# A new order for the first stage of a windowed-attention and feed-forward kernel: loads that wait for operations, short PE fills, casts on GpSimd, dilated parts split by chunk, and the last product cut in halves

## The chip, the cores and the metric

One core of one Trainium2 chip runs the whole program. The metric is the device time of one execution in microseconds (us). Three runs of the kernel before gave 823.49, 824.78 and 825.17 us, so the median is 824.78 us.

## The reference

The program computes attention inside windows and feeds its result through one gated layer.

```python
# q, k, v: 8 batches, 8 heads, 576 positions, 64 wide; float32
scores = (q @ k.T) / sqrt(64)
# heads 0-3: a query sees its own and the 31 positions before it ("plain")
# heads 4-7: it sees every 4th position among the last 128 ("dilated")
attn = softmax(where(mask, scores, -1e9)) @ v
x = attn.transpose(0, 2, 1, 3).reshape(4608, 512)
h = x @ w_in                       # 512 x 2048
g = h * clip(h + 3, 0, 6) / 6
out = g @ w_out                    # 2048 x 512
```

All products need more than one pass of a 32-bit float, so each of x, g, w_in and w_out is split into a high and a low part (an `fp32r` cast and a subtraction), and each product is the sum of high*high, high*low and low*high.

## The kernel before, in words

The attention is cut into 48 pieces, called trios here, t = 0 to 47. A trio holds 12 blocks of 32 queries of one batch, of plain or of dilated heads. For a trio the steps are: load its keys and queries (k) and its values (v); scores on TensorE (B); the row maximum (R), the subtraction (S) and the exponential (X); a transpose on TensorE (E) and its copy to SBUF (CA); the product with the values, which rides in a later B (FOLLOW, line 57: B3 carries the values of trio 1, B4 of 2, B5 of 3, B7 of 5, B8 of 6) or stands alone (V); the division by the row sum (Z, lines 327 to 341); a transpose back (Y) and its copy (CX, lines 389 to 394); and the split into high (XH, lines 468 to 474) and low parts (XL, lines 476 to 484). A column of tokens called a chunk has 384 of them. A plain trio is half of a chunk's plain heads; a dilated trio covers a third of the batch and so its results lie in several chunks, every fourth column (`spans`, lines 435 to 447).

Four chunks (0 to 3) go through an ordinary feed-forward: G is the first product of one chunk and one 128-wide slice f of the hidden layer (lines 563 to 575, 12 matmuls of 384 columns), RE and T the gate, GH and GL its high and low parts, H the second product (lines 625 to 637, 9 matmuls of 512 columns). The weights arrive as 64-bit numbers (w, one load for w_in and one for w_out of each f) and are converted by seven steps: U and Q on ScalarE, s, j and a on VectorE, h (the high part, lines 548 to 551) on ScalarE and l (the low part) on VectorE. The other tokens go through a scheme of fewer, larger products (lines 639 on), whose order a planner makes (`_in_time`, lines 1369 to 1471) from costs and due times.

The change is almost wholly in the first stage, whose order is written out by hand: the string ORDER (lines 58 to 80). Each word is one step, such as `B4` or `w0@R1`, and the four engines and the load queue that SyncE issues on each do their steps in the order of the string. `@R1` makes a load wait until that step is done (lines 1311 to 1315). ScalarE, VectorE and SyncE are held to the program's order (lines 1303 to 1305), TensorE too. G0, the first product of the feed-forward, can start when trios 0 to 4 are split and the first weights are converted.

D in the string is a fill: n products of zeros that nobody reads, each a float32 matmul of 384 columns, which keep TensorE at work where a wait is expected (lines 184 to 187). Eight bf16 products of zeros (lines 179 to 180) stand ahead of everything. The mask and a small 0/1 matrix come in one load, M0 (lines 799 to 803); every B begins with a matmul that reads both (line 355). A tile for k or v of trios 0 to 8 takes a slot of the general pool (lines 204 to 208).

At the other end, the last product of the last group (T4 in lines 1288 to 1294) is taken row block by row block: the last two of its sixteen steps run for rows 0 to 127 and then for rows 128 to 255, and each half is scaled by ScalarE (line 1150) and sent (line 1190).

```python
        if masked:
            _, kind, part = trios[ts]
            one, rows = (ident_b, P) if ts >= NFIRST else (spread, QB)
            nc.tensor.matmul(ps[:, :CH], lhsT=one, rhs=mask_of(kind, part, rows), start=True, stop=False)
```

Of the kernel before, what the change touches and what calls it, by code (L numbers as in the profile page):

```python
# [74 lines left out]
Q21 GL14 U21 j13 j12 G24 a13 RE7 a12 h13 T7 h12 l13 w22@l20 H14 GH7 RE24 l12 GL7 T24 G17 s21 Q22 j21 GH24 U22 GL24 a21
U23 G16 RE17 s22 s23 h21 T17 j22 GH17 G9 l21 w24@l12 Q24 a22 U24 j23 h22 H24 s24 l22 j24 w25@l22 a23 H15 RE16 GL17 h23
a24 RE9 T16 h24 l23 G26 GH16 T9 Q25 GL16 U25 l24 w27@GH16 GH9 s25 G19 j25 a25 H17 h25 Q27 l25 H16 RE26 GL9 w26@H17 k12
k13 v12 v13 M1 RE19 T26 T19 G21 GH26 GH19 Q26 H9 U26 s26 U27 j26 H7 RE21 GL26 a26 T21 h26 GL19 H5 GH21 l26 GL21 s27
j27 G23 a27 h27 H21 l27 RE23 T23 GH23 H19 GL23 H23
# [7 lines left out]
def windowed_attention_ffn(ctx: ExitStack, tc: tile.TileContext, qk, vp, w, mask, out, out_t):  # L87
# [100 lines left out]


    kqs, vs = {}, {}  # L190
    last = {}
    plan = []

    def in_turn(ins):

        for name in last.values():
            tc.add_manual_dep(
                ins.ins, name, mybir.DependencyInfo(mybir.DependencyClass.NoSync, mybir.DependencyReason.DATA), reason="in turn"
            )
# [10 lines left out]
    def load_qk(t):  # L210
        if t < T and t not in kqs:
            kqs[t] = load_tile(t, "kq", KW + CH)
            ins = nc.sync.dma_start(out=kqs[t], in_=qk[t].rearrange("h d x -> (h d) x"))
            if not plan:
                in_turn(ins)
            return ins
# [94 lines left out]
    def share(t):  # L311
        pv = pvs[t][:, : SLOTS * W].rearrange("p (s x) -> p s x", x=W)
        z = small.tile([P, SLOTS], F32, name="z")
        nc.vector.tensor_scalar_add(z, pv[:, :, D], 1e-9)
        nc.vector.reciprocal(z, z)
        pvs[t] = pv, z

    def shares(t, j):
# [5 lines left out]
        for i in (2 * j, 2 * j + 1):  # L324
            nc.scalar.mul(xs[t][:, i * D : (i + 1) * D], pv[:, i, 0:D], z[:, i : i + 1])
# [20 lines left out]
    def block(ts, tv, pools=()):  # L346
# [21 lines left out]
        last["block"] = product.ins.name  # L368
        return product

    def turn(src):
        ps = ps_a.tile([P, 512], F32, name="ps_a")
        for r in range(RT):
            ins = nc.tensor.transpose(ps[:, r * P : (r + 1) * P], src[:, r * P : (r + 1) * P], ident)  # L374
# [6 lines left out]
    def turn_x(t):  # L381
        tps["x", t], ins = turn(xs.pop(t))
        return ins
# [4 lines left out]

    def turned_x(t):
        xfs[t] = work_tile("xf")  # L390
        return nc.scalar.copy(
            xfs[t].rearrange("p (u i x) -> p i u x", u=2, x=QB),
            tps.pop(("x", t))[:, :CH].rearrange("p (i u x) -> p i u x", u=2, x=QB),
        )
# [73 lines left out]
    def high(t):  # L468
        b, kind, part = trios[t]
        assert b >= PLAIN or all(read[c] == NF for c in chunks(b - 2, kind, part) if b < 2 or c < PLAIN - 2)  # L470
        for src, view, plain in pieces_of(t):
            if plain:
                ins = nc.scalar.copy(view(xh), src)
# [34 lines left out]
    def load_w(p):  # L508
# [4 lines left out]
        in_turn(ins)  # L513
# [17 lines left out]
    def cv_shift(p):  # L531
        v = parts(p)[2]
        return nc.vector.tensor_scalar(
# [14 lines left out]
    def cv_high(p):  # L548
# [1021 lines left out]
```

## Time and profile before

| | |
|---|---|
| median of three runs | 824.78 us |
| the profiled execution | 829.52 us |
| its span, first to last instruction | 827.7 us |
| TensorE busy | 814.9 us (98%) |
| VectorE / ScalarE / GpSimd busy | 639.5 / 512.4 / 122.5 us |
| mean granted TensorE clock | 0.995 |
| B0 starts / G0 starts (from the span's start) | 4.85 / 41.54 us |
| last matmul starts | 823.55 us |

The profiled execution took 4.74 us more than the median of the runs. Times of single instructions below are from it. PE is TensorE, DVE VectorE, ACT ScalarE, POOL GpSimd, SP SyncE; "PEclk" is the granted share of TensorE's clock, where 1.00 is 2.4 GHz and 0.50 is 1.2 GHz. An idle time is given with what ended it; "issue" stands where the engine waited for nothing that the profile shows. B, E and the other step names are not in the profile: a step is found by its line and its place in the order of its engine.

### The profile page before, as it was taken

The numbers are of one execution on the slowest core, as the hardware profiler recorded it, in microseconds if no ns is written. First come the engines' busy times: TensorE is split into PE (matmuls) and PEld (weight loads), VectorE is DVE, ScalarE is ACT, GpSimd is POOL, SyncE is SP. The second block draws the span as 40 slices with busy tenths as digits, with TensorE's granted clock in tenths as the row PEclk, the third lists the DMA queues.
The fourth block names the chain that finished last, engine by engine and source line by source line (L and its number), as shares of the span: only waits on it lengthen the run. The fifth ranks groups of instructions, "written<-read, shape, count | busy, mean of one in ns | idle before, by whom it ended". The sixth has DMA issues, their size and how long they took to land.

```text
span 827.7 us, 20447 instructions
## 1 busy us (share of the span) xinstructions
PE 814.9 (98%) x8095; PEld 687.5 (83%) x8095; DVE 639.5 (77%) x1189; ACT 512.4 (62%) x1148; POOL 122.5 (15%) x268
## 2 busy tenths in 40 slices
PE   8799999999999999999999999999999999999998
PEld 5589989899888889878888888888888888888886
DVE  4699999568787998998989996575798934459943
ACT  3488776346877875677877565585565524446542
POOL 0000000013554454112360001031000000000000
PEclk9899999999999999999999999999999999999999
DMA  7847433336767879999985656786539369560632
GB/s 238 279 158 228 149 127 103 117 131 198 255 197 233 287 256 349 363 314 391 394 321 178 229 178 225 277 293 232 178 103 314 124 232 389 211 225 30 216 140 77
DMA packets 99343, 184.92 MB, mean 223 GB/s; under 512 B 6448, under 2 KB 35120, under 8 KB 99248
## 3 DMA queue, kind: packets, MB, share of 16 engines
q1 hardware_dynamic: 99248, 183.62, 64.4%
q8 instruction: 64, 1.05, 0.5%
q14 instruction: 31, 0.25, 0.1%
HBM read 144.79 MB, written 38.80 MB: 222 GB/s over the span
## 4 chain that ended last, share of the span: by engine, by line
PE 96%; ACT 2%; DVE 1%; issue 1%
PE ps_o L784 28%; PE ps_o L632 15%; PE ps_x L793 9%; PE ps_x L794 9%; PE ps_x L795 9%; PE ps_h L571 5%; PE ps_h L572 5%; PE ps_h L573 5%; PE ps_a L263 2%; PE ps_a L245 2%; PE ps_a L255 1%; PE ps_b L263 1%; PE ps_b L245 1%; PE ps_a L374 1%; PE idle L186 1%
## 5 line engine op out<-in xcount | busy, mean ns | idle before, releaser
L784 PE MATMUL ps_o<-gh,ring 128*128 128x512 f32 x672 | 182.5, 390 | 0.0
L784 PEld LDWEIGHTS ps_o<-gh,ring 128*128 128x128 f32 x672 | 126.2, 188 | 26.1
L1230 DVE TENSOR_TENSOR gl<-g,gh 128x512 fp32r<-128x512 f32 x168 | 109.1, 688 | 23.6 <-ACT gh L1226 17.8
L1226 ACT CAST gh<-g 128x512 fp32r<-128x512 f32 x168 | 97.0, 622 | 37.7 <-PE ps_o L784 36.8
L784 PE MATMUL ps_o<-gl,ring 128*128 128x512 f32 x336 | 103.8, 390 | 0.0
L632 PE MATMUL ps_o<-wo,gh 128*128 128x512 f32 x372 | 95.5, 392 | 0.0
L793 PE MATMUL ps_x<-cells,ring 128*128 128x512 f32 x240 | 94.1, 392 | 0.0
L795 PE MATMUL ps_x<-cells,ring 128*128 128x512 f32 x240 | 93.5, 390 | 0.0
L571 PE MATMUL ps_h<-x,wi 128*128 128x384 f32 x256 | 87.6, 342 | 0.0
L572 PE MATMUL ps_h<-x,wi 128*128 128x384 f32 x256 | 86.2, 337 | 0.0
L573 PE MATMUL ps_h<-x,wi 128*128 128x384 f32 x256 | 86.2, 337 | 0.0
L632 PEld LDWEIGHTS ps_o<-wo,gh 128*128 128x128 f32 x372 | 68.7, 188 | 11.5 <-DVE o L926 0.5
L784 PEld LDWEIGHTS ps_o<-gl,ring 128*128 128x128 f32 x336 | 63.1, 188 | 13.0
L794 PE MATMUL ps_x<-cells,ring 128*128 128x512 f32 x176 | 68.6, 390 | 0.0
L579 ACT ACTIVATE t<-ps_h,three 128x384 f32<-128x384 f32 x64 | 37.0, 581 | 41.0 <-PE ps_h L573 37.2
L794 PE MATMUL ps_x<-cell,ring 128*128 128x512 f32 x160 | 62.4, 390 | 0.0
L1198 DVE TENSOR_TENSOR g<-g 128x1024 f32<-128x1024 f32 x48 | 58.0, 1222 | 0.1
L586 POOL CAST gh<-t 128x384 fp32r<-128x384 f32 x36 | 24.4, 679 | 214.8 <-DVE t L582 200.0
L1095 DVE TENSOR_TENSOR g<-ps_x,g 128x512 f32<-128x512 f32 x48 | 33.1, 689 | 28.8 <-ACT g L1088 25.9
L1088 ACT COPY g<-ps_x 128x512 f32<-128x512 f32 x48 | 28.1, 586 | 42.6 <-PE ps_x L795 40.4
L793 PEld LDWEIGHTS ps_x<-cells,ring 128*128 128x128 f32 x240 | 45.1, 188 | 9.3
L795 PEld LDWEIGHTS ps_x<-cells,ring 128*128 128x128 f32 x240 | 45.1, 188 | 9.4
(137 smaller groups left out, 1665.3 us busy)
## 6 DMA issues: line engine op xcount, KB each, us to landing
ring<-sums SPq DMA_DIRECT2D x84, 512.0 KB, 8.6
ring<-rights SPq DMA_DIRECT2D x84, 512.0 KB, 4.8
st<-in_w SPq DMA_DIRECT2D x32, 512.0 KB, 4.4
kq<-in_qk SPq DMA_DIRECT2D x39, 416.0 KB, 4.6
v<-in_v SPq DMA_DIRECT2D x39, 390.0 KB, 5.8
sums<-wi SPq DMA_DIRECT2D x24, 256.0 KB, 6.8
rights<-wo SPq DMA_DIRECT2D x24, 256.0 KB, 6.1
out<-o SPq DMA_DIRECT2D x11, 512.0 KB, 3.3
```

The source lines that it names most:

```text
L571: nc.tensor.matmul(ph, lhsT=wt(f, 0)[:, ks], rhs=a, start=(kt == 0), stop=False)
L572: nc.tensor.matmul(ph, lhsT=wt(f, 0)[:, ks], rhs=b, start=False, stop=False)
L573: ins = nc.tensor.matmul(ph, lhsT=wt(f, 1)[:, ks], rhs=a, start=False, stop=(kt == NK - 1))
L579: return nc.scalar.activation(ts[n], phs[n], AF.Relu, bias=three, scale=1.0)
L632: ins = nc.tensor.matmul(po[c][tt], lhsT=g[:, tt * P : (tt + 1) * P], rhs=wt(f, row), start=(f == 0 and not i), stop=(f == NF - 1 and i == 2))
L784: nc.tensor.matmul(banks[part], lhsT=right[:, a, cols], rhs=x, start=(start and not i), stop=(i == 2), skip_group_check=True)
L793: nc.tensor.matmul(bank, lhsT=tile_[:, 0, ks], rhs=h[:, kt], start=(start and kt == 0), stop=False, skip_group_check=True)
L794: nc.tensor.matmul(bank, lhsT=tile_[:, 0, ks], rhs=l[:, kt], start=False, stop=False, skip_group_check=True)
L795: nc.tensor.matmul(bank, lhsT=tile_[:, 1, ks], rhs=h[:, kt], start=False, stop=(kt == 1), skip_group_check=True)
L1198: nc.vector.tensor_tensor(out=at[0], in0=at[1], in1=at[2], op=alu)
L1226: nc.scalar.copy(two[0], gated_tile(g, q, k))
L1230: nc.vector.tensor_tensor(out=two[1], in0=gated_tile(g, q, k), in1=two[0].bitcast(F32), op=ALU.subtract)
```

## The change

- ORDER is a new string. It has the same B, E, Y, V, G and H steps; of TensorE's real steps four neighbouring pairs swap places (E3 and Y2, Y9 and V10, H8 and H1, H25 and H18).
- The first loads are k0, k2, v0, k1, M0, v2, without a wait; before they were k0, M0, k1, k2, v0, k3, v1, v2. k3 now waits for R0 and v1 for X0. Later ones are tied anew: v3 to B4 (before j0), v5 to B5 (before XL2), k7 to l0 (before E6), k6 to XH0 (before E2), v6 to X6 (before j2). The hint of `in_turn` (lines 194 to 199), which tied loads in the program's order to the latest block and conversion without a wait, goes.
- The fills are bf16 matmuls of 512 columns, F, 14 in all; before there were nine D.
- 19 casts run on GpSimd instead of ScalarE: XH of four plain trios, eight h, six GH, and the high part of chunk 0. GpSimd is now held to the string's order too.
- The division of trios 3 and 5 is VectorE's reciprocal (Zs) and six ScalarE scalings (N) instead of VectorE's whole Z.
- Y writes its transposes already parted by head, so that CX is a plain copy. For a dilated trio CX puts its pieces straight into one tile for a chunk (`whole_x`), and the high part (P) and low part (L) are made once for the whole chunk, 768 columns, instead of three to five pieces for each trio.
- The last product: the second row block is taken in two halves of 256 columns, each with its own tile, scaling and transfer.

```diff
-k0 M0 k1 k2 v0 k3 v1 v2 B0 R0 S0 X0 D2 E0 B1 CA0 B2 R1 S1 w0@R1 X1 Z0 E1 k4@X1 R2 CA1 Y0 B3 S2 CX0 XH0 X2 XL0 Q0 U0
-E2 k6@E2 s0 Z1 CA2 D1 B4 R3 k5@R3 j0 v3@j0 S3 a0 w2@a0 X3 h0 Y1 Z2 B6 CX1 XH1 R4 Y2 R6 w4@R6 E3 CX2 XL1 CA3 S6 v4@S6
-XH2 D1 B5 S4 X6 XL2 v5@XL2 X4 Q2 l0 E6 k7@E6 U2 Z3 E4 CA6 R5 CA4 Y3 s2 D2 V4 CX3 k8@CX3 S5 XH3 j2 v6@j2 X5 XL3 Q4 D1
-E5 w13@E5 Z4 U4 CA5 a2 w6@a2 Y4 B7 s4 CX4 j4 h2 XH4 l2 v7@l2 D2 B8 Z5 R7 k9@R7 Y5 XL4 w7@XL4 CX5 Z6 G0 Q13 w1@Q13 XH5
...
+k0 k2 v0 k1 M0 v2 B0 R0 k3@R0 S0 X0 F3 v1@X0 E0 B1 CA0 B2 R1 w0@R1 k4@R1 S1 Z0 X1 E1 CA1 R2 Y0 B3 S2 CX0 XH0 k6@XH0 X2
+XL0 v4@XL0 Q0 U0 s0 F4 E2 Z1 CA2 k5@CA2 F4 B4 v3@B4 R3 j0 w2 a0 S3 X3 w4@X3 Y1 Z2 B6 CX1 pXH1 ph0 R6 R4 E3 k8@E3 F1 Y2
+CX2 CA3 XL1 S6 B5 v5@B5 S4 X6 v6@X6 X4 Q2 Zs3 l0 k7@l0 F1 E6 E4 U2 CA6 N3 CA4 F1 Y3 R5 s2 V4 CX3 j2 S5 X5 Q4 E5 w13@E5
+a2 Z4 CA5 w6@CA5 U4 Y4 CX4 B7 s4 j4 h2 pP0 B8 Zs5 v7@Zs5 L0 w7@Zs5 N5 k9@N5 Y5 CX5 Q13 R7 l2 S7 Z6 G0 X7 XH5 R8 XL5 Y6
...
+    def short_wait(n):
+        for _ in range(n):
+            ins = nc.tensor.matmul(idle, lhsT=zeros[:, :P], rhs=zeros[:, P : P + 512], start=True, stop=True)
+        return ins
...
+    def turn(src, apart=False):
...
+            to = ps[:, r * P : (r + 1) * P]
+            if apart:
+                to = ps[:, :CH].rearrange("p (u i x) -> p i u x", u=2, x=QB)[:, 2 * r : 2 * r + 2]
...
     def turned_x(t):
-        xfs[t] = work_tile("xf")
...
+        turned = tps.pop(("x", t))[:, :CH]
+        if not trios[t][1]:
+            xfs[t] = work_tile("xf")
+            return nc.scalar.copy(xfs[t], turned)
+        xu = turned.rearrange("p (u f) -> p u f", u=2)
+        for at, n, c, _, token in spans(t):
+            chunk, i = token // CH, token % CH // DIL
+            if chunk not in whole_x:
+                whole_x[chunk] = w_tile("raw", [2, CH])
+            to = whole_x[chunk].rearrange("p u (i c) -> p u c i", c=DIL)[:, :, c, i : i + n]
+            ins = nc.scalar.copy(to, xu[:, :, at : at + n])
+        return ins
+
+    def high_of(chunk, copy=nc.scalar.copy):
+        return copy(xh[chunk % 3][1], whole_x[chunk])
+
+    def low_of(chunk):
+        ins = nc.vector.tensor_tensor(out=xl[chunk % 3][1], in0=whole_x.pop(chunk), in1=xh[chunk % 3][1].bitcast(F32), op=ALU.subtract)
...
-                        for part in range(2):
+                        for part, xs in ((0, slice(0, CG)), (1, slice(0, HALF)), (1, slice(HALF, CG))):
                             for kk, two, after in waiting:
-                                x = multiply_op(p, kk, two, after, (part,))
-                            ends(p, x, (part,))
+                                x = multiply_op(p, kk, two, after, (part,), xs)
+                            last_piece(x, part, xs)
...
-        engines={mybir.EngineType.Activation, mybir.EngineType.DVE, mybir.EngineType.SP}
+        engines={mybir.EngineType.Activation, mybir.EngineType.DVE, mybir.EngineType.Pool, mybir.EngineType.SP}
```

## Rows read from the trace of the kernel before

**Rows 1.** Busy time by stretch of the span: length, then busy us and count of each engine, the granted clock, the DMA share and GB/s.

```profile
30.00:41.50 11.50, 9.10 (x208) 5.78 (x207) 5.51 (x15) 2.27 (x6) 0.00 (x0) 0.70 0.69 243
41.50:60.00 18.50, 17.86 (x415) 15.60 (x413) 17.29 (x41) 17.12 (x39) 0.00 (x0) 1.00 0.53 175
60.00:120.00 60.00, 60.00 (x354) 54.56 (x353) 56.52 (x112) 46.04 (x89) 0.00 (x0) 1.00 0.52 167
120.00:345.00 225.00, 224.95 (x2933) 201.25 (x2932) 184.58 (x393) 146.91 (x418) 75.83 (x149) 1.00 0.67 221
345.00:824.00 479.00, 478.37 (x3561) 394.69 (x3559) 358.59 (x589) 284.22 (x565) 45.61 (x111) 1.00 0.65 231
```

**Rows 2.** The chain that ended last, in the stretch from 27 to 42 us: start, length, what; two rows of idle time without a shown cause, and the longest fill (L186).

```profile
28.03 1.01 issue
...
32.91 2.40 issue
...
35.96 2.86 PE idle L186 x4
```

**Rows 3.** The page's list of DMA queues: the one that brings program code; packets, MB, share of 16 engines.

```profile
q8 instruction: 64, 1.05, 0.5%
```

**Rows 4.** Of TensorE's waits from 0 to 60 us, at its weight loads, the one for the mask: who, for whom, us in total, times, longest.

```profile
PEld L355 <- DMA mi<-in_mask: 0.8, 1, 0.8
```

**Rows 5.** The load queue's issues in the first 5 us, in order: start, length, what. L213 is k, L803 the mask, L222 v.

```profile
0.74 0.38 SPq L213 DMA_DIRECT2D first<-in_qk  x1
1.18 0.41 SPq L803 DMA_DIRECT2D mi<-in_mask  x1
1.64 0.89 SPq L213 DMA_DIRECT2D first<-in_qk  x2
2.58 0.43 SPq L222 DMA_DIRECT2D first<-in_v  x1
```

**Rows 6.** Time from issue to landing of three of these loads, each asked for alone: the first k, the mask, the first v.

```profile
DMA to landing us min/median/max: 3.3/3.3/3.3
...
DMA to landing us min/median/max: 3.4/3.4/3.4
...
DMA to landing us min/median/max: 6.3/6.3/6.3
```

**Rows 7.** Loads issued from 9 to 41 us: KB each, median us to landing.

```profile
first<-in_qk SPq DMA_DIRECT2D x5, 416.0 KB, 4.2
first<-in_v SPq DMA_DIRECT2D x5, 390.0 KB, 5.2
```

**Rows 8.** Busy time in the stretches of five blocks (columns as in rows 1): B0; B1; B3, with the values of trio 1; B8, with values, at the low clock; a V alone.

```profile
4.85:6.78 1.93, 1.93 (x51) 1.43 (x50) 0.00 (x0) 0.00 (x0) 0.00 (x0) 1.00 0.95 333
9.15:10.28 1.13, 1.13 (x51) 0.87 (x50) 0.00 (x0) 0.48 (x1) 0.00 (x0) 1.00 0.94 374
13.49:15.16 1.67, 1.67 (x99) 1.39 (x99) 0.97 (x2) 1.53 (x4) 0.00 (x0) 1.00 0.83 283
38.75:41.26 2.51, 2.51 (x99) 2.01 (x99) 0.00 (x0) 0.00 (x0) 0.00 (x0) 0.50 0.90 301
75.30:76.24 0.94, 0.94 (x50) 0.85 (x49) 0.92 (x2) 0.75 (x2) 0.00 (x0) 1.00 0.54 113
```

**Rows 9.** TensorE's time line, start and length: E0, the last products of B2, Y0.

```profile
8.70 0.52 PE L374 MATMUL ps_a<-ident,e 128*128 128x128 f32 x3 [0.20 <-ACT e L309]
...
11.60 0.28 PE L255 MATMUL ps_a<-first,a 64*32 64x65 f32 x2
...
13.04 0.52 PE L374 MATMUL ps_a<-ident,x 128*128 128x128 f32 x3 [0.39 <-DVE x L333]
```

**Rows 10.** Groups of instructions in the first 60 us: count, busy us, mean ns of one, idle time before them. L180 are the bf16 products of zeros, L186 the float32 fills, L387 CA. Then, from the time line (start, length), the three pieces of one dilated trio's XH and of its XL.

```profile
L186 PE MATMUL idle<-zeros 128*128 128x384 f32 x18 | 8.7, 600 | 0.0
L180 PE MATMUL idle<-zeros 128*128 128x512 bf16 x8 | 3.6, 632 | 1.3 <-DVE zeros L177 1.3
L387 ACT COPY a<-ps_a 128x384 f32<-128x384 f32 x11 | 5.2, 480 | 3.7 <-PE ps_a L374 3.6
...
26.91 0.91 ACT L473 CAST x<-xf 128x96 fp32r<-128x96 f32 x3
...
27.54 1.00 DVE L479 TENSOR_TENSOR x<-xf,x 128x96 fp32r<-128x96 f32 x3
```

**Rows 11.** A run of ten of ScalarE's scalings by the reciprocal (L325), from the time line: start, length. Then a group of VectorE by the page, sums of 1024 columns.

```profile
190.40 2.15 ACT L325 ACTIVATE x<-ps_a,z 128x64 f32<-128x64 f32 x10 [0.39 <-DVE z L315]
...
L1198 DVE TENSOR_TENSOR g<-g 128x1024 f32<-128x1024 f32 x48 | 58.0, 1222 | 0.1
```

**Rows 12.** The cast GH of 384 columns on GpSimd: ns of one, least/median/most, first and last start.

```profile
L586 POOL CAST gh<-t x36: 496/508/1437, 168.8 to 340.6; 128x384 fp32r<-128x384 f32 x36
```

**Rows 13.** VectorE's subtraction GL, which reads two tiles of SBUF: first from 40 to 150 us, where GpSimd is idle, then from 150 to 345 us, where it is at work.

```profile
L590 DVE TENSOR_TENSOR gl<-t,gh 128x384 fp32r<-128x384 f32 x24 | 13.3, 553 | 1.0 <-PE ps_o L632 1.0
...
L590 DVE TENSOR_TENSOR gl<-t,gh 128x384 fp32r<-128x384 f32 x40 | 22.4, 561 | 6.0 <-POOL gh L586 4.5 <-PE ps_o L632 0.9 <-ACT gh L586 0.6
```

**Rows 14.** The end: the last scaling of ScalarE, and the last two transfers with their time to landing.

```profile
823.98 0.60 ACT L1150 ACTIVATE o<-ps_o 128x512 f32<-128x512 f32 x1 [0.76 <-PE ps_o L784]
...
L1190 SPq DMA_DIRECT2D out<-o x2: 344/344/345, 823.2 to 824.6; - x2
...
DMA to landing us min/median/max: 2.0/2.0/2.1
```

More of the change, by code (lines that the diff above doesn't have):

```diff
@@ L212, in load_qk @@
             kqs[t] = load_tile(t, "kq", KW + CH)
[L213 to L216, printed above, removed]
+            return nc.sync.dma_start(out=kqs[t], in_=qk[t].rearrange("h d x -> (h d) x"))
     def load_v(t):
@@ L387, in turned_e @@
         return nc.scalar.copy(ats[t], tps.pop(("e", t))[:, :CH])
+    whole_x = {}
     def turned_x(t):
-        xfs[t] = work_tile("xf")
[L391 to L394, printed above, removed]
+        turned = tps.pop(("x", t))[:, :CH]
[9 more added lines that the diff above has]
+            ins = nc.scalar.copy(to, xu[:, :, at : at + n])
+        return ins
+    def high_of(chunk, copy=nc.scalar.copy):
+        return copy(xh[chunk % 3][1], whole_x[chunk])
+    def low_of(chunk):
+        ins = nc.vector.tensor_tensor(out=xl[chunk % 3][1], in0=whole_x.pop(chunk), in1=xh[chunk % 3][1].bitcast(F32), op=ALU.subtract)
+        written.update(trios[t] + (chunk,) for t in range(NFIRST) if trios[t][1] and chunk in chunks(*trios[t]))
+        return ins
     def turn_by_blocks(src, name):
@@ L472, in high @@
             if plain:
[L473 removed]
+                ins = copy(view(xh), src)
         return ins
@@ L564, in gemm1 @@
         c, f = steps[n]
-        assert 2 * f in converted and all(x in written for x in trios if c in chunks(*x))
+        assert 2 * f in converted and all(x in written or (*x, c) in written for x in trios if c in chunks(*x))
         read[c] += 1
@@ L784, in multiply_right @@
                 nc.tensor.matmul(
-                    banks[part], lhsT=right[:, a, cols], rhs=x, start=(start and not i), stop=(i == 2), skip_group_check=True
+                    banks[part][:, xs], lhsT=right[:, a, cols], rhs=x[:, xs], start=(start and not i), stop=(i == 2),
+                    skip_group_check=True,
                 )
@@ L1184, in seed, with ship @@
             return ops
-        def ship(name, after, part=slice(0, 2)):
+        def ship(name, after):
             def do():
@@ L1189, in do @@
                 to = out_t[2 * g + j, HALF * d : HALF * (d + 1), :].rearrange("(b p) x -> p b x", p=P)
-                nc.sync.dma_start(out=to[:, part], in_=os[name][:, part])
-            transfer(0.45, 1.0, do, after, gives=SLOT if part.stop == 2 else ())
+                nc.sync.dma_start(out=to, in_=os[name])
+            transfer(0.45, 1.0, do, after, gives=SLOT)
         def sum_of(name, to, x, y, alu, after, kk):
@@ L1235, in halves, with last_piece, do, send @@
             return two, [x, y]
-        def multiply_op(p, k, two, after, parts):
+        def last_piece(x, part, xs):
+            piece, (j, d) = [], HALF_OF["21"]
+            def do():
+                piece.append(w_tile("o", [xs.stop - xs.start]))
+                nc.scalar.mul(piece[0], banks[RIGHT_STEPS[T4][0]][part][:, xs], 1.0 / 6.0)
+            def send():
+                row = HALF * d + P * part
+                nc.sync.dma_start(out=out_t[2 * g + j, row : row + P, xs], in_=piece[0])
+            y = op("ACT", 0.35, do, [x], takes=SLOT)
+            transfer(0.45, 1.0, send, [y], gives=SLOT)
+        def multiply_op(p, k, two, after, parts, xs=slice(0, CG)):
             bank, at = RIGHT_STEPS[p][0], (2 * g + 1) * STREAM + RIGHT_TURNS.index((p, k)) // 2
@@ L1249, in multiply_op @@
                 [*after, ring_landed[at], *read_by.get(bank, ()), *(freed.pop(0) for _ in range(2 if start else 0) if freed)],
-                takes=[("ps_a", 2)] if start else (), gives=TWO if parts[-1] == 1 else (),
+                takes=[("ps_a", 2)] if start else (), gives=TWO if parts[-1] == 1 and xs.stop == CG else (),
             )
-            if parts[-1] == 1:
+            if parts[-1] == 1 and xs.stop == CG:
                 ring_step(at, x)
```

87 lines of the change are left out of this document (38 added, 49 removed).

## The prediction, made before the changed kernel was run

> **What bounds the kernel now.** Read first the busy times by stretch [rows 1]: from 60 us to the end TensorE is busy 60.00 of 60, 224.95 of 225 and 478.37 of 479 us. It is the bound there, and the planner's part, whose order the change leaves alone up to the last product, can give nothing. What is to be had lies ahead of 60 us and in the last 4 us. Between 41.5 and 60 us TensorE lacks 0.64 us of 18.5. So one time decides: when G0 starts. It is 41.54 us now, and whatever moves it moves the end, as long as VectorE, busy 17.29 of 18.5 and then 56.52 of 60 us, keeps up.
>
> Next the chain of waits from 27 to 42 us [rows 2]: a fill of 2.86 us stands on it and two idle times, 1.01 and 2.40 us, with no wait to explain them. They fall in the midst of a block, and the page lists 64 packets of program code, 1.05 MB in all [rows 3]: I read them as TensorE waiting for its program behind data in the DMA engines. In the same stretch the granted clock is 0.70 on average [rows 1]: part of it ran at 1.2 instead of 2.4 GHz.
>
> Then the start. B0's weight load waited 0.8 us for the mask [rows 4], so B0 already begins as early as its mask lets it.
>
> **The mask, moved from second to fifth load.** One DMA of 84 KB is moved past three loads on SyncE's queue: k2, v0 and k1. The loads are issued 0.44 us apart [rows 5]; k0 landed 0.74 + 3.3 = 4.1, the mask 1.18 + 3.4 = 4.6, v0 2.58 + 6.3 = 8.9 us [rows 5, 6], in the order of issue. v0 was fifth, behind k0, the mask, k1 and k2: the same five transfers that now end with the mask. So the mask lands at 8.9, and B0, which came 0.26 us after it, starts at 9.15 instead of 4.85 us: +4.3. The two ends are 4.6 (it overtakes) and 8.9; landings in order speak for the second.
>
> **From B0 to G0, step by step.** Durations are those of the old rows; only order and waits are new.
> - B0 takes 1.93 us again [rows 8], since TensorE has idled from the end of its eight products of zeros, about 4.9 us, on: 11.1. To E0 pass 8.70 - 6.78 = 1.92 us, R, S and X [rows 8, 9]: 13.0. F3 lies beside that.
> - E0, B1 and B2 take 0.52 + 1.13 + 1.67 = 3.3 us at full clock and, by the 1.93 and 2.51 of blocks that ran at half, about 5.2 at half. I take the middle, 4.2: 17.2. k3 and v1, issued at about 11.7 and 13.0, land in 4.2 and 5.2 us or less [rows 7], before they are used; w0 and k4 stand behind them on SyncE and are wanted at 21 and 23 us.
> - From B2's end (11.88) to Y0 (13.04) passed 1.16 us, the division Z0; Y0 itself takes 0.52 [rows 9]: 18.9. B3: 20.6.
> - F4, E2, F4. A bf16 fill took 3.6 / 8 = 0.45 us at the start [rows 10], about half at full clock, so four are 0.9. E2 waits for nothing by then, so these stand on the path: 22.9. B4: 24.6.
> - v3 now waits for B4. Its landing took 3.3 (first load, empty queue) to 5.2 us [rows 6, 7]; only k5 is ahead of it, so I take 3.6: 28.2. The other way to B5, through Z2, Y2, CX2 and CA3, ends at about the same time. B5: 29.9. w2, w4, k8 and v5 queue behind v3 on SyncE and land while the steps below run.
> - ScalarE then does U2 and CA6 and the six scalings N3, 0.215 us each [rows 11], 1.3, and CA4, 0.48 [rows 10]: 33.4. V4 0.94 [rows 8]: 34.4. Z4 and Y4, 1.7 as above: 36.1. v5 and k7 have landed by then.
> - CX4 in three pieces, 0.9 as XH had [rows 10]: 37.0. P0 on GpSimd: a cast of 384 columns took 0.50 to 1.44 us there, median 0.51 [rows 12], so 768 columns take between 0.9 and 2.9; the median holds, 1.0: 38.1. L0, 768 columns, from 1.22 us for 1024 [rows 11]: 0.95: 39.1.
> - Beside it B7 and B8, 2 x 1.67 from 36.1: 39.4, but Y5 waits for N5, six scalings after B7: 39.6 + 0.52 = 40.1.
> - Waits for program code: now 1.01 + 2.40 us [rows 2]. The loads are spread wider, so I keep 0.3; both ends, 0 and 3.4, stay in the range.
>
> G0 starts at 40.4, that is **-1.1 us**. What the fills took, 8.7 us busy [rows 10], and the code waits are gained; the mask takes 4.3 back.
>
> **Edits at nothing.** `in_turn` set no wait; taking it away leaves SyncE's order, which the string gives. Y writes the same columns to other places, and CX of a plain trio stays one copy of 384 columns; a contiguous one might gain 0.1 us, or nothing, beside other work of ScalarE. The new tiles for chunks take the places of `xf` tiles.
>
> **After G0.** TensorE's order hardly changes. Of the 0.64 us idle between 41.5 and 60 the wait ahead of V10 is now covered by Y9 (0.52): **-0.4**. VectorE loses work: six dilated trios had XL at 1.0 us each [rows 10], now three chunks at 0.95, and Z3 and Z5 give their multiplication to ScalarE, about 0.55 each: 4.2 us less by 90 us. None of it is on the path, it is cover. Casts that leave ScalarE, about 0.5 each, are hidden now too, since ScalarE is busy 46.04 of 60 us.
>
> GpSimd idles until 120 us. Its casts are slower than their median at times, 1.44 at most [rows 12], but apart from P0 and pXH1 a consumer stands at least one step further on. What do they cost VectorE? GL, which reads two SBUF tiles, took 553 ns with GpSimd idle and 561 ns with it at work [rows 13]: 8 ns each, nothing. The Trainium skill (SBUF — State Buffer, "Who interferes with whom") speaks against the change here: a VectorE instruction with two SBUF inputs and a GpSimd instruction that reads SBUF exclude each other for the whole instruction, and whoever comes first blocks the other. By the rows it is GpSimd that pays, up to 1.44 us for a cast of 0.51 [rows 12]; the sum goes by them.
>
> **The end.** The last scaling, 0.60 us for 512 columns [rows 14], becomes one of 256; with 0.215 for 64 columns that is about 0.4: -0.2. The transfer halves, 2.0 us to land now [rows 14], mostly not its size: -0.2, ends 0 and -0.5. Twelve matmuls of half the width replace six: nothing if they take half, +0.5 at worst. Sum **-0.3**.
>
> **Sum.** -1.1 - 0.4 - 0.3 = -1.8 us. The profiled execution took 829.52 us, 1.8 of it before and after its span; the median of the runs is 824.78, 4.74 lower, and I take the difference off the median: **823.0 us**. About 0.2%, 1.65 us, is what a measurement can tell, so this is barely a gain.
>
> **Rivals.**
> 1. *Slower: the clock stays low.* TensorE idles from 4.9 to 9.15 us, and fills of 14 x 0.225 = 3.2 us replace 8.7. If it runs at 1.2 GHz through B4 and again at B7 and B8, then B3, B4, B7 and B8 cost 0.84 more each, two F4 1.8, E2 0.3: 5.5, of which 0.5 is slack: **828.0**. For it: B8 took 2.51 us at 0.50 after 2.4 us of idling, B3 with the same products 1.67 at 1.00 [rows 2, 8], and the chain above leaves TensorE idle for half of 30 to 36 us. Against: from 13 to 24 us it is nearly always busy. It decides if the first rise comes after B4, about 24 us. Chance 0.27.
> 2. *Faster: the mask costs little*, being small, or B0's delay is lost in later waits. G0 at 36.1: **818.7**. Against it stand the landings in order. Chance 0.13.
> 3. *No difference.* Only B7 and B8 run at half clock (+1.7), or code waits stay: **824.7**. Chance 0.15.
> 4. *GpSimd holds VectorE up.* If each of 19 casts blocks VectorE for its 0.51, that is 9.7 us against 4.2 saved, and 41.5 to 120 us has only 4.7 us of idle VectorE: TensorE starves for 0.8 and G0's gain goes: **824.9**. This is how the page's rule above would tell. Against: 8 ns [rows 13]. Chance 0.05.
>
> **Numbers.** The forecast has 0.40: 0.30 over 0.2% faster, 0.10 within, its own range 821 to 825. Faster 0.30 + 0.13 = 0.43; same 0.10 + 0.15 + 0.05 = 0.30; slower 0.27. The range goes from rival 2 to rival 1, 818.5 to 828.0; what lies beyond is a clock that is low throughout (another 1.6) or code waits on top.
>
> **What would show it.** Right: the mask lands near 9 us and B0 follows; no fill over 1 us after 25 us; v3 lands within 4 us of B4's end; G0 at 39.5 to 41; then no idle TensorE up to 60 us; GL still near 0.55 us; the last scaling near 0.4. Wrong: B0 before 7 us (rival 2), blocks of 2.5 us at a clock of 0.50 between 13 and 25 us (rival 1), idle without a cause within B5, V4 or B7 (rival 3), or gaps ahead of H after 45 us that wait for VectorE (rival 4).

## The result, and the profile of the changed kernel

The changed kernel took 833.81 us, the median of four runs (831.27 to 836.43); beside it the kernel before took 824.13 us (823.32 to 825.17). The ratio is 1.0107, interval 1.0088 to 1.0125: slower by about 9 us (9.7 by the medians), where 823.0 was forecast, and beyond the range. The execution profiled below is its fastest, 831.27 us with a span of 829.5, so what it shows is the least of the loss.

The start went as the prediction said, and it is there that most is lost. First the load queue's issues in the first 5 us of the changed kernel (start, length, what; L816 is the mask), which answer [rows 5]:

```profile
0.74 0.86 SPq L210 DMA_DIRECT2D first<-in_qk  x2
1.65 0.42 SPq L216 DMA_DIRECT2D first<-in_v  x1
2.11 0.43 SPq L210 DMA_DIRECT2D first<-in_qk  x1
2.59 0.43 SPq L816 DMA_DIRECT2D mi<-in_mask  x1
```

Then, from the list of loads up to 45 us, the mask with its time to landing, and what TensorE waited for in that time (us in total, times, longest):

```profile
mi<-in_mask SPq DMA_DIRECT2D x1, 84.0 KB, 6.5
```

```profile
PE ps_a L351 <- DMA mi<-in_mask: 4.2, 1, 4.2
PE idle L191 <- issue: 2.0, 1, 2.0
...
PE ps_a L249 <- ACT a L385: 1.0, 1, 1.0
```

84 KB, issued at 2.59, landed 6.5 us later, behind the four loads issued ahead of it. In second place it took 3.4 [rows 6]. B0's weight load, which waited 0.8 us in [rows 4], waits 5.1 here, and TensorE's products stand idle for 4.2 of it. The busy times by stretch (columns as in [rows 1]) show TensorE at rest from 4.9 to 9.1 us, and the stretches that [rows 1] has:

```profile
4.90:9.10 4.20, 0.01 (x1) 0.00 (x0) 0.00 (x0) 0.00 (x0) 0.00 (x0) 1.00 0.79 284
9.10:13.00 3.90, 3.33 (x52) 1.68 (x53) 1.11 (x2) 0.52 (x1) 0.00 (x0) 1.00 0.07 13
13.00:30.00 17.00, 13.38 (x479) 9.43 (x484) 10.40 (x24) 7.40 (x17) 1.06 (x2) 1.00 0.84 264
30.00:41.50 11.50, 10.38 (x319) 7.35 (x308) 7.57 (x18) 8.72 (x28) 1.21 (x1) 0.86 0.77 244
...
60.00:120.00 60.00, 58.38 (x340) 51.82 (x340) 56.57 (x105) 37.55 (x70) 9.92 (x13) 1.00 0.45 151
```

Three things are to be seen. From 30 to 41.5 us the granted clock is 0.86: part of it ran at 1.2 GHz again. From 60 to 120 us TensorE lacks 1.62 us, where [rows 1] had none. And ScalarE gave 8.5 us of that stretch to GpSimd (46.04 to 37.55), but VectorE's 56.52 stayed at 56.57: the cover of 4.2 us that the prediction saw does not appear there (where it went is told below, under GpSimd and VectorE).

Three blocks of the changed kernel by stretch, B0, B3 and B7:

```profile
9.15:11.08 1.93, 1.93 (x50) 1.43 (x51) 0.00 (x0) 0.00 (x0) 0.00 (x0) 1.00 0.01 3
17.90:19.50 1.60, 1.60 (x98) 1.34 (x98) 0.89 (x2) 1.56 (x4) 0.00 (x0) 1.00 0.90 322
36.99:38.70 1.71, 1.59 (x89) 1.26 (x88) 1.12 (x2) 1.56 (x5) 0.70 (x1) 1.00 0.75 177
```

B3 and B7 took 1.60 and 1.71 us, so the blocks of 2.5 us that would speak for rival 1 are not in this execution. The 1.00 in B0's row is not its speed: it took 1.93 us, as in [rows 8], where B1 did the same products in 1.13.

The chain that ended last, up to 45 us (start, length, what), against [rows 2]:

```profile
9.15 0.50 PE ps_a L351
...
13.00 0.52 PE ps_a L372 x3
...
17.36 0.52 PE ps_a L372 x3
...
19.47 0.97 PE idle L191 x4
20.44 0.33 PE ps_a L372 x3
20.77 0.86 PE idle L191 x4
...
25.36 2.00 issue
27.35 0.38 PE idle L191
...
34.47 0.98 PE ps_a L249 x46
```

B0 starts at 9.15 and E0 at 13.00, both as forecast; Y0 at 17.36 (18.4 forecast, 17.2 and Z0's 1.16), V4 at 34.47 (33.4). In between stands an idle time of 2.00 us without a wait. G0 starts at 41.39, not at 40.4.

Further on, TensorE's waits from 95 to 120 us, and what VectorE and GpSimd did ahead of them, from the time line (start, length):

```profile
PE ps_o L644 <- ACT wo L563: 1.0, 1, 1.0
PE ps_h L583 <- DVE t L594: 0.4, 1, 0.4
```

```profile
102.54 1.28 DVE L560 CUSTOM_DVE_ANT_0 va<-va 128x1024 uint16<-128x1024 uint16 x2
...
103.94 0.61 POOL L563 CAST wo<-va 128x512 fp32r<-128x512 f32 x1 [5.39 <-ACT va L543]
104.50 0.61 POOL L563 CAST wi<-va 128x512 fp32r<-128x512 f32 x1
104.59 1.07 DVE L568 TENSOR_TENSOR wo<-va,wo 128x512 fp32r<-128x512 f32 x1 [0.77 <-POOL wo L563]
```

The subtraction l15 stands directly behind its own cast ph15 and waits 0.77 us for it, then takes 1.07 us beside the next cast; 0.68 is usual (below). T18 queues behind it, and G27 behind T18.

The end, from the time line, against [rows 14]:

```profile
824.12 0.60 ACT L1260 ACTIVATE o<-ps_o 128x512 f32<-128x512 f32 x1 [7.99 <-PE ps_o L796]
...
825.19 0.38 ACT L1260 ACTIVATE o<-ps_o 128x256 f32<-128x256 f32 x1 [0.47 <-PE ps_o L796]
...
825.62 0.38 PE L796 MATMUL ps_o<-gh,ring 128*128 128x256 f32 x1 [0.47 <-ACT o L1260]
...
826.28 0.38 ACT L1260 ACTIVATE o<-ps_o 128x256 f32<-128x256 f32 x1 [0.71 <-PE ps_o L796]
```

The last scaling is 0.38 us, near the 0.4 forecast. But the second half's products go to the bank that the first half's scaling is reading, and they wait 0.47 us for it.

Where each profiled execution spent its time, from the starts of the steps on TensorE's time line (us; "to end" is H23 to the span's end). The kernels are those of the next section.

| profiled execution | B0 | G0 | G0 to H10 | H10 to H11 | H11 to H23 | to end |
|---|---|---|---|---|---|---|
| before (829.52) | 4.85 | 41.54 | 61.9 | 8.21 | 51.5 | 664.5 |
| changed (831.27) | 9.15 | 41.39 | 62.6 | 10.42 | 51.5 | 663.5 |
| before, again (829.29) | 4.85 | 41.59 | 61.4 | 8.21 | 51.5 | 664.8 |
| before, the last product in halves (825.63) | 4.85 | 38.02 | 62.2 | 8.21 | 51.5 | 663.9 |
| before, two loads later (824.15) | 4.57 | 37.02 | 61.8 | 8.21 | 51.5 | 663.8 |
| before, H18 behind H25 (825.68) | 4.85 | 37.66 | 61.8 | 8.21 | 51.5 | 664.7 |
| before, three fills of nine (824.08) | 4.49 | 36.81 | 62.1 | 8.21 | 51.5 | 663.6 |
| before, mask fifth (832.05) | 9.74 | 44.66 | 61.8 | 8.21 | 51.5 | 664.1 |
| changed, mask second (828.19) | 4.85 | 38.95 | 62.6 | 9.42 | 51.5 | 663.9 |
| the same, old order later (823.78) | 4.84 | 36.01 | 62.6 | 8.21 | 51.5 | 663.6 |

### The profile page after: what moved, and what is told of

It reads as the page before. It is cut to its first block, busy times and chain, and to the rows that moved or that the text cites. A ratio compares the mean times of both kernels' runs of the same rounds, so it can differ in the third digit from the quotient of the medians.

```text
span 829.5 us, 20448 instructions
## 1 busy us (share of the span) xinstructions
PE 812.6 (98%) x8097; PEld 685.2 (83%) x8097; DVE 638.5 (77%) x1172; ACT 505.4 (61%) x1139; POOL 135.5 (16%) x287
## 4 chain that ended last, share of the span: by engine, by line
PE 94%; DVE 2%; DMA 2%; ACT 1%; issue 1%; SPq 0%; POOL 0%; ACTq 0%; DVEq 0%
PE ps_o L796 28%; PE ps_o L644 15%; PE ps_x L806 9%; PE ps_x L808 9%; PE ps_x L807 9%; PE ps_h L583 5%; PE ps_h L585 5%; PE ps_h L584 5%; PE ps_a L257 2%; PE ps_a L239 2%; PE ps_b L257 1%; PE ps_a L249 1%; PE ps_b L239 1%; DMA mi<-in_mask 1%; DMA kq<-in_qk 1%
## 5 line engine op out<-in xcount | busy, mean ns | idle before, releaser
L796 PE MATMUL ps_o<-gh,ring 128*128 128x512 f32 (+1 forms) x676 | 182.8, 388 | 0.5 <-ACT o L1260 0.5
L796 PE MATMUL ps_o<-gl,ring 128*128 128x512 f32 (+1 forms) x338 | 104.2, 388 | 0.0
L427 POOL COPY a<-a_t 32x192 f32<-32x192 f32 x72 | 31.0, 431 | 142.5 <-DVE a L420 124.1
```

Source lines behind the costliest of these rows:

```text
L796: nc.tensor.matmul(banks[part][:, xs], lhsT=right[:, a, cols], rhs=x[:, xs], start=(start and not i), stop=(i == 2), skip_group_check=True,)
```

## The experiments

The theory after the result: the mask's place costs the 4.3 us and more, and the profiled execution of before hid that, since it was itself a late one. The rivals: the casts on GpSimd, the fills that went, the loads tied to operations, the later order, the last product.

**The kernel before once more.** No edit.

> The kernel before, unchanged, profiled once more. The profiled execution that the prediction was summed from took 829.52 us, 5 us over the median of the runs. Theory 1 (that execution was not a typical one): the new profile has no idle time of 2.4 us within B7 and little or no stretch at 1.2 GHz, and its G0 starts near 36 to 37 us instead of 41.54; the span is near 822.5. Theory 2 (profiling itself costs the 5 us, evenly or at the start): G0 starts near 41.5 again, the span is near 827.7 while the times stay near 824.

Measured: 825.33 us, ratio 0.9995 (0.9985 to 1.0004). Its profile fell on the longest of its 12 runs, 829.29 us. It shows again the idle time of 2.40 us and the long fill of [rows 2], and a low clock from 30 to 41.5 us (chain of waits, then the busy times by stretch):

```profile
28.02 1.06 issue
...
32.95 2.40 issue
...
36.00 2.86 PE idle L186 x4
```

```profile
30.00:41.50 11.50, 9.10 (x208) 5.75 (x208) 5.51 (x15) 2.27 (x6) 0.00 (x0) 0.70 0.74 246
```

All 122 comparison runs of the kernel before have medians of 825.4 to 826.1 by chip, and a highest of 829.69. So [rows 2] are rows of its slowest executions. By itself this run is what theory 2 foretold: G0 at 41.59, a span of 827.5, and the other runs near 825.3. No profile of the unedited kernel in a usual execution was taken. Against theory 2 stand three profiles below, of kernels with this first stage or almost this one: 824.15 to 825.68 us, G0 at 37.0 to 38.0.

**The mask, each way.** In the changed kernel back to second place; in the kernel before to fifth.

```diff
-k0 k2 v0 k1 M0 v2 B0
+k0 M0 k2 v0 k1 v2 B0
...
-k0 M0 k1 k2 v0 k3 v1 v2 B0
+k0 k1 k2 v0 M0 k3 v1 v2 B0
```

> The changed kernel with one thing undone: the first loads are k0, M0, k2, v0, k1, v2. Theory 1 (the mask's place decides): B0 starts at 4.9 us instead of 9.15 and everything up to G0 follows, so 4 us or more of the 9.7 us come back: 829 to 830. Rival (other waits set G0, the delay of B0 is slack): under 1.5 us come back, 832.5 to 834.

> The kernel before with one thing done: the first loads are k0, k1, k2, v0, M0, k3, v1, v2. Theory 1: B0 starts at 9.15 us, the end moves by 4.3: 828.4. Rival (slack behind B0): under 1.5 us, 824 to 825.5.

Measured: the changed kernel falls to 827.69 us, ratio 1.0018 (1.0006 to 1.0031). The kernel before rises to 831.35, ratio 1.0070 (1.0053 to 1.0088), which is 5.8 us of 825.74. Its stretches from 4.9 us on, and the wait:

```profile
4.90:9.10 4.20, 0.02 (x1) 0.00 (x0) 0.00 (x0) 0.00 (x0) 0.00 (x0) 0.98 0.93 305
9.10:13.00 3.90, 3.26 (x51) 2.20 (x52) 1.11 (x2) 0.08 (x1) 0.00 (x0) 0.50 0.48 185
13.00:30.00 17.00, 14.53 (x470) 9.78 (x473) 11.05 (x28) 9.24 (x21) 0.00 (x0) 0.92 0.54 169
```

```profile
PE ps_a L355 <- DMA mi<-in_mask: 4.8, 1, 4.8
```

So the mask's place alone makes 0.7 of the 1.07%. In this profile the mask took 7.1 us to land and B0 started at 9.74, 4.9 us later than in that of before; and after the standstill B0 and what follows run at 1.2 GHz, a granted clock of 0.50 up to 13 us.

**The last product in halves, in the kernel before.** Only the functions of the last product, as in the change.

> The kernel before with only the last product cut in halves. Prediction's term: -0.3 us. By the changed kernel's trace (TensorE idles 0.47 us ahead of the last half until the scaling of the first half has read the bank): +0.2 us. Rival: no difference beyond 0.1 us.

Measured: 825.43 us, ratio 1.0000 (0.9985 to 1.0015). Neither gain nor loss can be seen. Its profile, 825.63 us, shows the first stage of before in a usual execution (TensorE's idle times without a wait up to 45 us, then the busy times of the stretch in [rows 1]):

```profile
PE ps_a L255 <- issue: 2.2, 3, 1.1
...
PE ps_a L245 <- issue: 1.3, 1, 1.3
```

```profile
30.00:41.50 11.50, 10.10 (x229) 7.67 (x229) 8.96 (x23) 5.47 (x13) 0.00 (x0) 1.00 0.78 261
```

The idle times of [rows 2] are here too, 1.1 and 1.3 us in place of 1.01 and 2.40. But the clock stays at 1.00, and G0 starts at 38.02.

**Casts back to ScalarE**, with the mask second: first the eight of weights (as ph15 and ph30 here), then all.

```diff
-a30 a15 ph15 l15 G11 ph30
+a30 a15 h15 l15 G11 h30
```

> The changed kernel with the mask second again, and the eight weight casts h back on ScalarE, at the same places of the order. With the mask alone undone 0.18% over the kernel before were left, and its trace has H25 waiting 0.9 us and the steps about it 2.0 us late, behind l15, which waits on VectorE right behind a cast of GpSimd. Theory (GpSimd's weight casts and their contention with VectorE cause this): the steps from H10 to H11 are no longer late, 1.0 to 2.0 us less than with the mask alone undone, that is 0.1% faster to equal with the kernel before. Rival (the order causes it: l15 stands right behind its own cast, whichever engine makes it): the lateness stays, no difference beyond 0.5 us.

> As the run before, with all 19 casts on ScalarE. Theory (the casts on GpSimd are worth nothing or less): no slower than with the eight alone put back, within 0.5 us. Rival (the other eleven, P0 and those of x and of the gate, relieve ScalarE where it is the limit): 1 us or more slower, seen as TensorE waiting on ScalarE's copies between 20 and 60 us.

Measured: 1.0016 (0.9997 to 1.0036) and 1.0019 (1.0005 to 1.0033), against 1.0018 with the casts on GpSimd. H10 to H11 still takes 10.4 and 9.9 us. So the casts do not cause that delay, and no gain shows in the time, though the intervals leave room for 1 us.

**Three loads earlier**, with the mask second.

```diff
-k5@CA2 F4 B4 v3@B4 ... S6 B5 v5@B5 S4 X6 v6@X6 X4 ... l0 k7@l0
+k5@CA2 v3@CA2 F4 B4 ... S6 v5@S6 B5 S4 X6 v6@X6 k7@X6 X4 ... l0
```

> The changed kernel with the mask second again, and v3, v5 and k7 no longer tied to the blocks B4, B5 and the step l0, but to CA2, S6 and X6 ahead of them. Theory (the chain block, load, block sets G0): B5 and B7 start earlier by 1 us or more, the time is 1 us or more below that with the mask alone undone. Rival (code waits: more loads in flight keep the program code waiting, so what B5 gains B7 gives back): the unexplained idle time ahead of or within B7 stays at 2.4 us or more, and the time is the same within 0.5 us.

Measured: 1.0017 (1.0001 to 1.0033). The ties of these loads cost nothing that can be seen. The profile has G0 at 36.67; that of the mask second alone, with an idle time of 3.5 us without a wait, had it at 38.95. The times do not show these 2.3 us.

**Two loads later, in the kernel before.**

```diff
-CX3 k8@CX3 S5 ... j2 v6@j2 X5 ... E5 w13@E5
+CX3 S5 ... j2 X5 ... E5 k8@E5 v6@E5 w13@E5
```

> The kernel before with k8 and v6 tied to E5 instead of CX3 and j2, some 4 us later. In its profile the packet of program code at 33.06 us began when v6 had landed, and B7 stood idle from 32.91 to 35.32 us. Theory (that code waits behind the loads k8 and v6): the idle time within B7 falls from 1.3 to 2.4 us to under 0.6, the code packet starts near 30 us; no stretch at 1.2 GHz follows; B8 may wait up to 1 us for v6; in sum 0.5 to 2 us faster, and fewer slow executions. Rival (the idle time has another cause, or B8 waits for what B7 gains): the idle time in B7 stays, or the sum is 0 to 1 us slower.

Measured: 1.0001 (0.9988 to 1.0013). Its profile (824.15 us) is one of a short execution. It has an idle time without a wait as well, but of 1.58 us, the clock stays up, and G0 starts at 37.02 (busy times by stretch, then the chain of waits):

```profile
30.00:41.50 11.50, 9.39 (x227) 7.48 (x226) 8.71 (x21) 6.04 (x15) 0.00 (x0) 1.00 0.91 321
```

```profile
31.71 1.58 issue
33.70 1.49 PE idle L186 x4
```

The time did not fall. Nor is 1.58 us a shorter idle time than usual: where these loads were not moved it took 1.30 us (the halves) and 1.58 us (H18, next). The 2.40 us belonged to the long executions. So the two loads do not set this wait, and whether it costs the median anything is not shown, since no edit took it away.

**H18 ahead of H25**, with the mask second; and the reverse in the kernel before.

```diff
-h29 G27 s18 l29 ... ph18 GL27 l18 H18 H11
+h29 G27 H18 s18 l29 ... ph18 GL27 l18 H11
...
-h29 s18 H18 l29 ... GL27 l18 w10@Q18
+h29 s18 l29 ... GL27 l18 H18 w10@Q18
```

> The changed kernel with the mask back in second place, and with H18 moved from behind H25 to directly behind G27, where the order of before has it. With the mask alone moved back the ratio to before was 1.0018, and in every run of the new order 1.6 to 2.5 us were lost between the starts of H10 and H11 (9.9 to 10.8 us, where the old order took 8.21): H25 waited about 1.0 us for weight 29's conversion on ScalarE. Theory: the order is what is left; H18 fills H25's wait, the idle 1.0 us ahead of H25 goes, H10 to H11 takes 8.5 to 9.5 us, and the ratio falls by about 0.13% to 1.0005 (0.999 to 1.002). Rival: ScalarE and VectorE are simply late there, so whatever TensorE does next waits for them: then a wait of about 1 us turns up ahead of H18, H11 or G22 instead, and the ratio stays at 1.0018.

> The kernel before with one edit: H18 moved from ahead of l29 to behind l18, so that TensorE comes to H25 first, as in the changed order. Theory: H25 then waits about 1.0 us for weight 29's conversion, H10 to H11 takes 9.0 to 9.7 us instead of 8.21, and the ratio is 1.0010 (1.0002 to 1.0018). Rival: in the old order h29 and l29 are early enough, H25 waits for nothing, and the ratio is 1.0000.

Measured: in the first the waits are gone and H10 to H11 takes 8.21 us, but the ratio is 1.0038 (1.0018 to 1.0059), not 1.0005. In the second H25 waits for nothing (8.21 us), ratio 1.0011 (0.9999 to 1.0023). So H25's place alone is not the cause, and a wait of a microsecond taken out of one profile did not move the median: the runs of the first go from 825.29 to 834.46. The clock alone does not part them: the one of 834.46 us had a mean clock of 0.996, one of 829.95 had 1.000.

**Fills while the mask is awaited**, in the changed kernel.

```diff
-k0 k2 v0 k1 M0 v2 B0
+k0 k2 v0 k1 M0 v2 F11 B0
```

> The changed kernel as it is, with eleven bf16 fills (0.45 us each at half clock) ahead of B0, so that TensorE multiplies from 4.9 us until the mask lands instead of standing idle. Theory: the mask's place costs more than its 4.3 us because the standstill also keeps the clock low: it rose at 12.8 us there and at 4.8 to 7.2 us in the runs with the mask second. Then B0 still starts at 9.2 to 10 us, the clock rises before it, B0 takes 1.1 us instead of 1.93, the steps to B3 gain 1.5 to 2.5 us together, and the time is 1.5 to 2.5 us below the changed kernel's: ratio 1.0080 (1.007 to 1.009) to before. Rival: the path to G0 is set by loads and by ScalarE and VectorE, not by TensorE's clock: G0 stays where it was and the ratio stays at 1.010 to 1.011.

Measured: 833.2 us, ratio 1.0086 (1.0068 to 1.0103), against 1.0107 (1.0088 to 1.0125), measured apart. The intervals overlap, so the times show no gain. The profile shows the mechanism: after 3.2 us of products of zeros, B0's forty-eight products take 0.88 us instead of 1.50, E0 starts at 12.20 instead of 13.00, and G0 at 40.65 instead of 41.39.

```profile
9.14 0.33 PE L351 MATMUL ps_a<-mi 32*128 32x384 bf16 x1 [1.20 <-DMA mi<-in_mask]
9.40 0.88 PE L239 MATMUL ps_a<-first 64*32 64x64 f32 x48
...
12.20 0.52 PE L372 MATMUL ps_a<-ident,e 128*128 128x128 f32 x3 [1.17 <-ACT e L303]
```

**The old order behind the first stage**, with the mask second: from L2 on, near 60 us, all that is left in the order of before, its casts on ScalarE. It was run twice.

> The changed kernel with the mask second, and from the subtraction L2 (about 60 us) on all that is left in the order of before, with its casts on ScalarE; the first stage, its casts on GpSimd, its parts by chunk and the last product in halves stay as changed. Theory: what is left of the loss with the mask second (0.18%, 1.5 us) lies in the order between 95 and 110 us: H10 to H11 then takes 8.2 to 8.5 us, G0 to H23 about 121.5 us, and the ratio is 0.9995 (0.998 to 1.001). Rival: it lies in the first stage (code waits of 0.8 to 3.5 us, the chain to G0): then H10 to H11 falls to 8.2 but the ratio stays at 1.0015 or more, with G0 at 38 us or later.

> The kernel with the mask second and the old order behind the first stage once more, beside the one with more fills: ratio 1.0019 as the first time (1.000 to 1.0037), with about a third of the runs at a mean clock of 0.995 or less and near 830 us. If none is that low here, the comparison with more fills tells nothing of the clock.

Measured: 1.0019 (1.0000 to 1.0037), then 1.0002 (0.9989 to 1.0015). Neither reading is excluded by these two alone. But the runs fall apart by their mean granted clock: four and three of twelve are at 0.995 or less, with medians of 830.2 and 827.5 us; the others have 825.0 and 825.0.

**More fills in that kernel, and fewer in the kernel before.**

```diff
-X0 F3 v1@X0 ... E3 k8@E3 F1 Y2 ... l0 F1 E6 ... CA4 F1 Y3
+X0 F6 v1@X0 ... E3 k8@E3 F3 Y2 ... l0 F3 E6 ... CA4 F3 Y3
...
-D2 E0 ... D1 B4 ... D1 B5 ... D2 V4 ... D1 E5 ... D2 B8
+D1 E0 ... B4 ... B5 ... D1 V4 ... E5 ... D1 B8
```

> The kernel of the run with the mask second and the old order behind the first stage, with more bf16 fills in the first stage: six instead of three ahead of E0, three instead of one ahead of Y2, E6 and Y3. Of that kernel's 12 runs eight had a mean granted clock of 0.996 or more and a median of 825.0 us, four had 0.992 to 0.994 and a median of 830.2: time and clock go together (correlation -0.88). Theory: what is left of the loss is TensorE standing idle where the change took 8.7 us of fills away and put 3.2 us in: then the mean clock is 0.998 or more in nearly all runs, the median 825 us, the ratio 0.9995 (0.998 to 1.001). Rival: the fall comes from idle time without a wait within a block (program code), which no fill covers: then three or four of the runs are at 0.992 to 0.995 again, and the fills, nine more at 0.2 to 0.45 us, partly on the path, bring the ratio to 1.0025 or more.

> The kernel before with its six groups of fp32 fills cut: each of two becomes one, each of one goes (three fills in place of nine, 5.8 us less busy in the profiled execution). Theory: the fills keep the clock up, so a third of the runs or more fall to a mean clock of 0.996 or less (on these chips one of 93 runs of the kernel before had 0.995, none less) and take 828 to 831 us; the median of all rises, ratio 1.001 to 1.003. Rival: the fills stand on the path and the clock falls by code waits alone: then the time falls by up to 2 us, ratio 0.998 to 0.9995, with the clock as before.

Measured: 1.0003 (0.9992 to 1.0015) with more fills, none of twelve runs at 0.995 or less; 1.0015 (0.9998 to 1.0031) with fewer, and seven of twelve that low. In the profile of the second the clock is 0.70 from 13 to 30 us, where the profiled execution of before has 1.00:

```profile
13.00:30.00 17.00, 14.44 (x406) 11.12 (x405) 12.53 (x31) 11.06 (x26) 0.00 (x0) 0.70 0.73 232
```

The clocks of all runs, by what the first stage has, say it more plainly than the medians:

| first stage | runs at 0.995 or less | at 0.996 or less |
|---|---|---|
| before | 3 of 122 | 6 of 122 |
| before, again and with edits that keep mask and fills (four kernels) | 1 of 46 | 3 of 46 |
| before, three fills of nine | 7 of 12 | 9 of 12 |
| new, mask second (six kernels, one of them twice) | 24 of 83 | 37 of 83 |
| of these, the old order behind it, twice | 7 of 24 | 10 of 24 |
| the same, nine fills more | 0 of 12 | 4 of 12 |

That the fills keep the clock up is shown in the kernel before. In the new first stage it hangs on where the line is drawn: at 0.995 the nine fills more take the low runs away, at 0.996 they do not. And a low clock is not yet lost time: the profiled execution with three fills, at 0.50 from 18 to 24 us, has G0 at 36.81 and took 824.08 us, the second shortest of its twelve. That the fills are worth the whole rest is not shown: the two intervals for the time take in 1.0000.

## Why the prediction was wrong

**The step that failed is the last one of the sum: the difference to the profiled execution was taken off the median.** The text knew that this execution was 4.74 us above the median. It then counted as gains the very things that made it so: its idle time of 2.40 us, its long fill, its blocks at half clock [rows 1, 2]. Usual executions do not lose most of that: in three profiles of 824 to 826 us of kernels with that first stage or almost that one (the halves alone, two loads later, H18 moved), the clock stays at 1.00 and G0 starts at 37.0 to 38.0, not at 41.54. Idle times without a wait they have as well, 1.06 and 1.30 us in the first; these are no mark of the long executions. Against those profiles the forecast G0 of 40.4 is a loss of 2.4 to 3.4 us, not a gain of 1.1. With no other step changed, the forecast would have been 824.78 + 2.4 to 3.4 - 0.7, which is 826.5 to 827.5 us: slower. A gain that a run makes only now and then can't be set against a cost that every run pays.

Forecast and median lie 10.8 us apart. Of these, 7.3 lie between profiled execution and median: 4.74 were taken off, while the changed kernel's profiled execution stands 2.5 below its own median. What its longer executions lose no trace shows; the longest, 836.43 us, had a mean clock of 0.998. The other 3.5 are terms of the sum, from one profiled execution to the other, where each came out against its forecast by about: G0 +1.0, after G0 +3.3, the end -0.7.

**The mask: mechanism right, size short.** It landed at 9.1 (8.9 forecast) and B0 followed at 9.15, as forecast to the hundredth; there is luck in that, since B0 came 0.1 us after the landing and not 0.26. Priced alone in the kernel before, its place costs 5.8 us, not 4.3: there B0 started 4.9 us late, and then at 1.2 GHz. In the profiled execution of the changed kernel the standstill cost no more than forecast up to E0. Rival 1, fewer fills and a clock that stays low, came nearest with 828.0 us and a chance of 0.27. But its sign is absent there: B3, between 13 and 25 us, and B7 ran at full clock, and only in the stretch from 30 to 41.5 was part of the time low (0.86). Two of the other three runs had mean clocks of 0.991 and 0.993 and may have been its case. What part of the loss it is stays open.

**From B0 to G0: close.** Each step up to 24 us came 0 to 1.3 us early. Lost were the 2.00 us without a wait (0.3 kept, 3.4 as the upper end), so G0 came 1.0 us late. (The step to 33.4 also holds 1.7 us for U2 and CA6, for which the prediction gives no price.) For such idle times the Trainium skill (Runtime: NRT & Kernel Launch, "Instruction fetch mechanics") says that crossing a 16 KiB block of program is mostly hidden. If these idle times are such crossings, the rows do not agree for this stage of small products: 2.00, 2.40, 1.58 and 3.50 us stand idle there with no wait. That program code is the reason was only a reading. The traces support it: the idle times stand 256 apart, within one, in the count of TensorE's products and weight loads (705, 1217 and 1473 in the profile of before, 961 and 1474 in that of the changed kernel), whatever the step there. And each ends 0.9 to 1.5 us after a 16 KB packet of the instruction queue: the one of 2.40 us at 35.31, the packet at 34.03; the one of 2.00 us at 27.36, the packet at 25.94. No run settles it: with k8 and v6 moved the wait stayed.

**After G0: wrong.** Forecast was -0.4. From G0 to H23 the changed kernel took 124.6 us, the profiled before 121.6. About 2.2 of the 3 us lie between H10 and H11. The sentence that a consumer stands at least one step behind each cast was untrue for ph15: l15 follows directly. Yet with that cast on ScalarE the delay stayed, and with H18 moved it went but the time did not follow. With the old order put back, H10 to H11 is 8.21 us in all three profiles, and the runs above a mean clock of 0.995 have medians of 825.0 to 825.3 us; with the new order four of five kernels have theirs at 827.1 to 828.2, the fifth at 825.5 (on chips where the medians of before lie up to 0.7 us apart). This speaks for 1 to 2 us in the later order. Which of its moves costs them is open.

**GpSimd and VectorE.** The sum took 8 ns for each GL. From 40 to 150 us of the changed kernel, and for the usual l on the same line (wi, then wo), against [rows 13]:

```profile
L602 DVE TENSOR_TENSOR gl<-t,gh 128x384 fp32r<-128x384 f32 x24 | 14.1, 587 | 1.8 <-PE ps_o L644 1.1 <-ACT gh L598 0.5
...
L568 DVE TENSOR_TENSOR wi<-va,wi 128x512 fp32r<-128x512 f32 x14 | 9.6, 683 | 0.0
```

587 ns instead of 553: 34 ns each, 0.8 us in all, and l15 once 1.07 for 0.68. That is the sharing that the Trainium skill (SBUF — State Buffer, "Who interferes with whom") describes, so VectorE pays too, which the sum denied. With all casts back on ScalarE GL takes 552 ns again. The pages give what it came to, VectorE's busy time in all: 639.5 us before (638.9 to 639.9 in its variants), 638.5 in the changed kernel, 635.6 with the casts back. So 3.9 of the 4.2 us of work went as forecast, and the 19 casts put 2.9 back. But the runs with casts on ScalarE have the same ratio as those with casts on GpSimd: rival 4 is out as the cause of what is left with the mask second.

**The end: nothing.** -0.3 was forecast, 1.0000 (0.9985 to 1.0015) measured, an interval too wide to tell 0.3 us. The scaling shrank as said; the 0.47 us wait on the shared bank was not in the sum.

**What of the 1.07% is explained:** 0.7 (alone) to 0.9 (taken back) by the mask's place; about 0.2 is left with the mask second, in which low clocks for want of fills and the order after 60 us may both have a part; these runs can't divide it.

## What to carry to other kernels

Before a difference is taken off a median, ask which rows of the profiled execution its other executions don't have: here a stretch at half clock and the length of one idle time, but not the idle times themselves. A kernel with an edit far away serves as a second profile of the stage. A small load that the first product needs stays at the head of its queue: every run pays for its landing. Products of zeros that look like waste in a busy-time table may be what holds the clock: count the runs at a low clock before cutting them, and look at the time as well, since the two did not always go together here.

## What was not expected of the hardware

- A load of 84 KB landed 3.4 us after its issue in second place, and 6.5 and 7.1 us after it in fifth, behind four loads.
- The same kernel's executions differ by up to 7 us (822.96 to 829.68 on one chip), and time and mean granted clock go together: correlation -0.79 over these 29 runs, 0.86 us for each 0.001 of the clock. In the other three groups of runs of that kernel it is -0.67 to -0.70, 0.62 to 0.75 us.
- Three fills in place of nine (2.7 us of them in the profile, against 7.1 in that of the kernel with two loads later) made the kernel no faster: seven of its twelve runs had a clock of 0.990 to 0.994.
- TensorE stood idle without a wait for up to 3.5 us, at places 256 of its instructions apart, and each time until shortly after a 16 KB packet of the instruction queue.
